# A scan-then-experts kernel: decays loaded first, bf16 filler matmuls, a reordered chunk pipeline, earlier gathers, and a GpSimd drain moved

## The chip, the cores and the metric

The kernel runs on one core of a Trainium2 chip. The time is device microseconds of one execution of the whole program; of several runs the median is taken. TensorE (PE, with its weight loads PEld), VectorE (DVE), ScalarE (ACT) and GpSimd (POOL) are the engines; SyncE (SP) and ScalarE issue plain DMAs, GpSimd issues the indirect ones (gathers and scatters by a list of row numbers). Each engine runs its own instructions in order and waits for the others through semaphores.

## What is computed

A chunked state-space scan (4 batches, 8 heads, 768 positions, head size 32, state size 16), whose output rows, 3072 of 256, go to a router and then to one of 8 experts each:

```python
for c in range(nc):                      # the reference's chunks
    L = np.exp(cum[..., :, None] - cum[..., None, :]) * causal
    y_intra = (C @ B.T * L) @ x
    y_inter = (C @ state) * exp(cum)[..., None]
    state = decay_full * state + sum_j(B_j x_j * decay_from_j)
x = y as rows (3072, 256)
logits = normed(x) @ normed(expert_emb).T / tau
e = argmax(logits); gate = softmax(logits)[e]
out[mask_e] = gate * (relu(x[mask_e] @ w1[e]) @ w2[e])   # 256 -> 1024 -> 256
```

## The kernel before

The order of every engine's work is written by hand, in the order of the Python calls (`tc.manual_schedule`); the framework adds only the semaphores. All data are float32, except some counting matrices in bfloat16.

**Set-up** (`mamba`, lines 624 to 652). `expert_emb` (416) issues two small loads on ScalarE's queue, `load_decays` (40) six loads of 16 KB, three each on SP's and ScalarE's queues; `load(k, 0)` (49) starts chunk 0's inputs on SP. `build_consts` (77) fills constants with VectorE memsets and GpSimd selections. `warm_up` (126) issues 12 float32 matmuls of 128 columns whose result nobody reads. `decays` (131) is a string of some ten small VectorE operations that turn the decay factors into running products `f`, for chunks 0 to 3 (half 0) or 4 and 5 (half 1). `spread_decays` (155) multiplies `f` out on TensorE into columns 384 to 512 of the PSUM tile `pg`; `scale_c` (215) multiplies C by it on VectorE, giving `cp`; `split_b` (207) and `mask_c` (225) make masked copies of B and `cp` on ScalarE. `inverses` (185) takes reciprocals of `f` (VectorE, then two ScalarE copies); `turn_inverses` (194) transposes them on TensorE into `rT`, by which GpSimd scales x (`scale_x`, 239, and `scale_first_half`, 249). `block_ends` (165) and `spread_ends` (173) spread the decays at block ends; `square_emb`, `scale_emb` (439) and `turn_emb` (454) make the normed expert embedding, and `route_consts` (464) the constants of the routing on GpSimd.

**The scan** goes over 6 chunks of 128 positions, all batches and heads at once (`for c in range(NC)`, 654 to 733). For chunk c:
- `inner(c, 0)` and `inner(c, 1)` (317): products of B and C into `pg`, for two batches each. `mask_inner` (333) multiplies them by the causal mask on VectorE into `g` (1.76 us each). There is one `pg`: the second half's products wait for VectorE to have read the first half, and, as the tile is shared, also for `scale_c` of the next chunk.
- `finish(c-1)` (392) turns the outputs of the chunk before into rows and appends the router's logits; `keep_rows` (402) copies them on ScalarE, `send_rows` (410) stores them in DRAM.
- `pick(c-2)` (501), five VectorE operations, finds each row's expert; `count_picks` (517) counts them on GpSimd; `rank_rows` and `keep_ranks` (522, 540), `places` (545) and `locate` (584) turn counts into row lists per expert.
- `from_states` (343), `outputs(c, 0)`, `outputs(c, 1)` (354), `first_outputs` (372): matmuls that add up the chunk's output in `py`; `keep_outputs` (385) copies it on ScalarE.
- `sums` (294), `add_sums` (306), `decay_states` (278): the state for the next chunk; `between` (260) and `pass_c` (231) are small GpSimd steps for it.

In chunk 5 the row lists of chunks 0 to 2 are already known: `gather_halves` (808) gathers the first rows of experts 0 and 1 (four indirect DMAs), `early_jobs` (855) makes two jobs of them, and `scan_end` (737) weaves their matmuls among the last routing steps.

**The experts** (`moe`, 1010). A job has `turn_x` (900, transposes), eight `up` (916), two `down` (930) and one `out` (945) per 104 rows: two transposes, a scaling by the gate on VectorE, and a scatter by GpSimd. The loop's last job does its `up`s and returns at line 1038; `leftover` (1149) then handles rows beyond an expert's 416, in a branch that is not taken here; `moe_end` (1068) does the last job's `down`s and four `out`s, with a `gpsimd.drain()` after the second of them (line 1077). A drain makes GpSimd's sequencer wait until its work is done.

Of the kernel before, what the change touches and what calls it, by code (L numbers as in the profile page):

```python
# [17 lines left out]
Q = 128  # L18
# [57 lines left out]

def build_consts(k):
    nc, pool, mc = k.nc, k.const, k.mc
    k.heads = mc.tile([128, Q], F32, name="heads")
    nc.vector.memset(k.heads[:], 0.0)  # L80
    nc.vector.memset(k.heads[:, 0:Q:SQ], 1.0)
    k.ready = mc.tile([128, 1], F32, name="ready")
    nc.scalar.activation(k.ready[:], k.heads[:, 0:1], ACT.Square)
    k.spread = mc.tile([128, 4, 128], F32, name="spread")
    nc.gpsimd.memset(k.spread[:], 0.0)
    for b in range(NB):
        s = k.spread[32 * b : 32 * b + 32].rearrange("k c (q t n) -> k c q (t n)", q=4, t=2)
        for t in range(2):
            nc.gpsimd.affine_select(
                out=s[:, :, :, N * t : N * t + N], in_=s[:, :, :, N * t : N * t + N],  # L90
                pattern=[[-1, 4], [-4, 4], [0, N]], compare_op=ALU.not_equal, fill=1.0, base=-16 * t,
                channel_multiplier=1,
            )
    k.tmask = mc.tile([128, 2], F32, name="tmask")
    nc.vector.memset(k.tmask[:], 0.0)
    for q in range(4):
        nc.vector.memset(k.tmask[32 * q : 32 * q + N, 0:1], 1.0)
    nc.vector.tensor_scalar(
        out=k.tmask[:, 1:2], in0=k.tmask[:, 0:1], scalar1=-1.0, scalar2=1.0, op0=ALU.mult, op1=ALU.add
    )  # L100
    k.of_b = mc.tile([128, NB], F32, name="of_b")
    nc.vector.memset(k.of_b[:], 0.0)
    for b in range(NB):
        nc.vector.memset(k.of_b[32 * b : 32 * b + 32, b : b + 1], 1.0)
    k.ident = pool.tile([128, 128], F32, name="ident")
    make_identity(nc, k.ident[:])
    k.mask = mc.tile([128, 3 * HQ], F32, name="mask")
    nc.gpsimd.memset(k.mask[:], 1.0)

    def keep(m, pattern, base):  # L110
        nc.gpsimd.affine_select(
            out=m, in_=m, pattern=pattern, compare_op=ALU.is_ge, fill=0.0, base=base, channel_multiplier=-1
        )

    keep(k.mask[0:HQ, 0:HQ], [[1, HQ]], 0)
    keep(k.mask[HQ:, 0:HQ], [[1, HQ]], 0)
    keep(k.mask[:, HQ:].rearrange("p (v i) -> p v i", v=2), [[0, 2], [1, HQ]], HQ)
    k.xb = [mc.tile([128, NB, 4, 2, D], F32, name=f"xb{i}") for i in range(2)]
    for t in k.xb:
        nc.vector.memset(t[0:HQ, :, :, 1, :], 0.0)  # L120
        nc.vector.memset(t[HQ:, :, :, 0, :], 0.0)
    k.half = pool.tile([128, NT], F32, name="half")
    nc.gpsimd.memset(k.half[:], 0.5)


def warm_up(k):
    for _ in range(12):
        k.nc.tensor.matmul(k.pz[0][:, 0:Q], lhsT=k.heads[:], rhs=k.heads[:], start=True, stop=True)


def decays(k, kk):
# [185 lines left out]
def inner(k, c, j):  # L317

    t = k.ld[c]
    for u in range(2):  # L320
        b = 2 * j + u
        for lhsT, rhs, a, n in ((t.bi[:, b, :], t.cp[:, b, 3:5, :], HQ, Q), (t.bt[:, b], t.cp[:, b, 0, :], 0, HQ)):
            for q in range(4):
                r = slice(32 * q, 32 * q + 32)
                m = lhsT[r] if n == Q else lhsT[r].rearrange("p v s -> p (v s)")
                x = rhs[r].rearrange("p v s -> p (v s)") if n == Q else rhs[r]
                k.nc.tensor.matmul(  # L327
                    k.pg[:, q, 192 * u + a : 192 * u + a + n], lhsT=m, rhs=x, start=True, stop=True,
                    tile_position=(32 * q, 0),
                )  # L330
# [133 lines left out]
def route_consts(k):  # L464
    nc = k.nc

    def ints(name, shape, pattern, base, by, dtype=F32):
# [8 lines left out]
    k.place_at = ints("place_at", [128, TR], [[1, TR]], 1, 0)  # L476
    k.first_of = ints("first_of", [128, NT], [[TR, NT]], 0, 0)
    k.ints = ints
    ones = k.mc.tile([128, 128], F32, name="ones")
    nc.gpsimd.memset(ones[:], 1.0)  # L480
    before = k.mc.tile([128, 128], F32, name="before")
    nc.gpsimd.affine_select(
        out=before[:], in_=ones[:], pattern=[[1, 128]], compare_op=ALU.is_gt, fill=0.0, base=0,
        channel_multiplier=-1,
    )
    k.ones = k.const.tile([128, 128], BF16, name="ones_b")
    nc.gpsimd.tensor_copy(out=k.ones[:], in_=ones[:])
    k.before = k.const.tile([128, 128], BF16, name="before_b")
    nc.gpsimd.tensor_copy(out=k.before[:], in_=before[:])
    k.ob = k.const.tile([128, NU, E], BF16, name="ob")  # L490
    k.pre = k.const.tile([128, NU + 1, E], BF16, name="pre")
    nc.gpsimd.memset(k.pre[:, 0, :], 0.0)
# [131 lines left out]
def mamba(k):  # L624
# [6 lines left out]
    for c in range(NC):  # L631
        k.ld[c] = Net()
        k.ld[c].g = []
    expert_emb(k)
    load_decays(k)
    load(k, 0)
    build_consts(k)
    warm_up(k)
    decays(k, 0)
    load(k, 1)  # L640
    square_emb(k)
    route_consts(k)
    spread_decays(k, 0)
    split_b(k, 0)
    inverses(k, 0)
    scale_c(k, 0)
    mask_c(k, 0)
    block_ends(k, 0)
    turn_inverses(k, 0, k.py[:, 0, 0:256])
    scale_emb(k)  # L650
    scale_x(k, 0, nc.gpsimd)
    scale_first_half(k, 0, nc.gpsimd)

    for c in range(NC):
        t = k.ld[c]
        n = c + 1
        if c + 2 < NC:
            load(k, c + 2)
        if c in (3, 4):
            load_weights(k, 0, (c - 3,))  # L660
        if c == 5:
            load_weights(k, 1, (0,))
        if n < NC:
            spread_decays(k, n)
        if 0 < c < NC - 1:
            add_sums(k, c)
        inner(k, c, 0)
        mask_inner(k, c, 0)
        if c == NC - 1:
            early_places(k, c - 3)  # L670
        elif c >= 3:
            locate(k, c - 3)
            keep_located(k, c - 3)
        if n < NC:
            scale_x(k, n, nc.gpsimd)
        if c >= 2:
            pick(k, c - 2)
        if n < NC:
            scale_c(k, n)
        if c == 0:  # L680
            spread_ends(k, 0, k.pz[0][:, 0:48])
            turn_emb(k, k.pz[1][:, 400:416])
        if c > 0:
            finish(k, c - 1)
            keep_rows(k, c - 1)
            send_rows(k, c - 1)
        if c == 1:
            spread_ends(k, 1, k.pz[0][:, 400:424])
        inner(k, c, 1)
        mask_inner(k, c, 1)  # L690
        if c == 0:
            sums(k, 0)
            add_sums(k, 0)
        if n < NC:
            split_b(k, n)
            mask_c(k, n)
        if c >= 2:
            count_picks(k, c - 2)
        if n < NC:
            scale_first_half(k, n, nc.gpsimd)  # L700
            if c in (0, 3):
                between(k, n, 4 if c == 0 else NC)
            pass_c(k, n)
        if 3 <= c < NC - 1:
            add_located(k, c - 3)
        if c == NC - 1:
            k.early_x = gather_halves(k, k.gi0, 0, 3 * NB * Q)
        if c == 0:
            decays(k, 1)
            block_ends(k, 1)  # L710
            inverses(k, 1)
        if c > 0:
            from_states(k, c)
        if c >= 2:
            rank_rows(k, c - 2)
            keep_ranks(k, c - 2)
        outputs(k, c, 0)
        outputs(k, c, 1)
        if c == NC - 1:
            early = early_jobs(k)  # L720
            early[0].turn_x()
        first_outputs(k, c)
        keep_outputs(k, c)
        if c + 2 < NC:
            sums(k, n)
        if c == 1:
            turn_inverses(k, 1, k.pz[0][:, 0:256])
        if c >= 2:
            places(k, c - 2)
        if c == 4:  # L730
            shift_places(k)
        if n < NC:
            decay_states(k, n)
    return early


def scan_end(k, early):
# [2 lines left out]
    c = NC - 1  # L740
    first, second = early
    gates = Gates(k, k.ep, k.early_x, TR, NT)
    pick(k, c - 1)
    count_picks(k, c - 1)
    first.up(0)
    rank_rows(k, c - 1)
    keep_ranks(k, c - 1)
# [57 lines left out]
    k.gi0 = gi  # L805


def gather_halves(k, gi, t, rows=T):
    x = k.ep.tile([TR, 2 * HT, KD * Y1], F32, name="xg", tag="xg", bufs=2)
    for e in range(2):  # L810
        for i in range(HT):
            gather(k, x[:, HT * e + i, 0:W], gi[:, NT * e + t + i : NT * e + t + i + 1], rows)
    return x


def gather(k, x, at, rows=T):
# [48 lines left out]


def late_jobs(k):
    x = k.late_x = gather_halves(k, k.gi, HT)
    jobs = []
    for e in range(2):  # L870
        j = Job(k, HT, TR, k.w1t[e], k.w2t[e], k.ep, k.next_bank)
# [138 lines left out]
def moe(k, second, late):  # L1010
# [10 lines left out]
    for i in range(E):  # L1021
# [5 lines left out]
        for f in range(KF):  # L1027
# [8 lines left out]
            if i >= 4 and f >= 5:  # L1036
                next(left, None)
        if i == E - 1:
            return j
        if x is not None:  # L1040
            gates.power()
# [26 lines left out]
def moe_end(k, j):  # L1068

    for i in range(2):  # L1070
        j.down(0, i)
        if i:
            j.out(0)
        j.down(1, i)
        if i:
            j.out(1)
            k.nc.gpsimd.drain()
    j.out(2)
    j.out(3)

# [244 lines left out]
```

## Time and profile before

| what | us |
|---|---|
| median of 6 runs (294.32 to 300.26) | 298.5 |
| the profiled execution's own time | 298.41 |
| its span, first to last instruction | 296.6 |
| TensorE busy in the span | 267.7 (90%) |
| VectorE, ScalarE, GpSimd busy | 118.8, 70.8, 123.9 |
| expert layers at full TensorE load | about 114.5 to 271.3 |
| TensorE's granted clock, mean | 0.945 |

A page cuts the span into 40 slices and gives each engine's busy share in tenths, and the share of its full clock that TensorE was granted. Groups of instructions come with count, busy time and the mean of one, and with the idle time just before them and what ended it. "issue" is time in which an engine waited for nothing that the profile shows. A "q" after an engine's name is its sequencer, which handles waits, branches and drains.

### The profile page before, as it was taken

What the parts mean: (1) busy time and instruction counts of PE and PEld (TensorE: products, weight loads), DVE (VectorE), ACT (ScalarE), POOL (GpSimd) and SP (SyncE); (2) the same over time, 40 slices, a digit from 0 to 9 for tenths busy, and PEclk for the clock granted to TensorE, in tenths of its full rate; (3) what the DMA queues carried; (4) which work ended last, traced back from release to release, by engine and by line L of the source; (5) the groups of instructions that cost most, each with busy time, mean ns of one, the idle gap of its engine ahead of it and who ended that gap; (6) DMA issues with size and microseconds to landing.
All of it is one profiled execution on the core that took longest, in us unless ns stands there. A gap on an engine that the chain in (4) does not pass through costs nothing.

```text
span 296.6 us, 5877 instructions
## 1 busy us (share of the span) xinstructions
PE 267.7 (90%) x2331; PEld 199.7 (67%) x2331; DVE 118.8 (40%) x350; ACT 70.8 (24%) x211; POOL 123.9 (42%) x173
## 2 busy tenths in 40 slices
PE   6879967998789999999999999999999999999920
PEld 6769856887579999999555565565555555556920
DVE  6675575558625412143250441242244046042120
ACT  3315335051136132340310130130031031010000
POOL 8987346452521561845251263155057051031012
PEclk9578999599979999999999999999999999999995
DMA  4993779517316950698644527429321010011011
GB/s 136 283 322 90 239 231 223 177 61 160 105 32 204 250 134 0 150 245 195 176 102 101 167 78 148 144 56 201 124 71 47 15 43 6 0 29 33 2 29 28
DMA packets 22302, 35.86 MB, mean 121 GB/s; under 512 B 2547, under 2 KB 15550, under 8 KB 22272
## 3 DMA queue, kind: packets, MB, share of 16 engines
q1 hardware_dynamic: 19024, 28.73, 35.3%
q0 software_dynamic: 3072, 6.67, 9.1%
q8 instruction: 19, 0.31, 0.5%
q14 instruction: 11, 0.09, 0.1%
q10 hardware_dynamic: 176, 0.06, 0.1%
HBM read 29.05 MB, written 6.65 MB: 120 GB/s over the span
## 4 chain that ended last, share of the span: by engine, by line
issue 43%; PE 27%; POOL 16%; DVE 8%; DMA 3%; POOLq 1%; ACT 0%; ACTq 0%
POOL xg L817 8%; POOL out_dram L952 7%; PE pg L327 5%; DVE g L337 4%; PE eb L922 4%; PE eb L937 4%; PE py L378 3%; DMA out_dram<-yo,to 3%; PE py L365 3%; PE pz L298 1%; PE py L348 1%; PE hp L922 1%; PE pg L159 1%; DVE cp L220 1%; POOL gr L979 1%
## 5 line engine op out<-in xcount | busy, mean ns | idle before, releaser
L922 PE MATMUL hp<-xT,w 128*128 128x416 f32 (+1 forms) x256 | 83.9, 469 | 0.0
L937 PE MATMUL yp<-hT,w 128*128 128x416 f32 (+1 forms) x288 | 80.1, 436 | 0.3 <-PEq L1157 0.3
L952 POOL DMA_INDIRECT out_dram<-yo,to x32 | 32.5, 1016 | 100.8 <-DVE yo L951 90.6
L937 PEld LDWEIGHTS yp<-hT,w 128*128 128x128 f32 x288 | 52.3, 190 | 24.8 <-issue 23.1
L922 PEld LDWEIGHTS hp<-xT,w 128*128 128x128 f32 x256 | 45.8, 190 | 23.2 <-issue 23.1
L817 POOL DMA_INDIRECT xg<-y_rows,gi x32 | 35.4, 1106 | 12.7 <-issue 8.4
L926 ACT ACTIVATE hT<-hp 128x416 f32<-128x416 f32 (+1 forms) x32 | 15.2, 475 | 81.9 <-PE hp L922 80.2
L928 DVE TENSOR_SCALAR hT<-hp 128x416 f32<-128x416 f32 (+1 forms) x32 | 17.2, 538 | 40.4 <-PE hp L922 38.5
L337 DVE TENSOR_TENSOR g<-pg,mask 128x1536 f32<-128x1536 f32 x12 | 21.1, 1758 | 16.2 <-PE pg L327 16.1
L943 DVE COPY yoT<-yp 128x416 f32<-128x416 f32 (+1 forms) x9 | 4.4, 489 | 48.7 <-PE yp L937 48.7
L327 PE MATMUL pg<-cp,bi 32*128 32x128 f32 x192 | 13.1, 344 | 3.1 <-DVE cp L220 3.1
L519 POOL TENSOR_TENSOR pre<-pre,ob 128x8 bf16<-128x8 bf16 x24 | 4.8, 200 | 25.7 <-DVE ob L514 24.2
L979 POOL TENSOR_TENSOR gr<-gr,half 104x4 f32<-104x4 f32 x8 | 8.7, 1092 | 16.2 <-ACT sq L973 16.1
L365 PE MATMUL py<-g,xs 128*32 128x64 f32 x384 | 10.8, 247 | 3.5 <-issue 2.9
L378 PE MATMUL py<-g,xb 128*64 128x64 f32 x192 | 10.0, 261 | 4.2 <-issue 4.2
L973 ACT ACTIVATE sq<-xg 104x256 f32<-104x256 f32 x32 | 13.0, 409 | 0.0
L922 PE MATMUL eb<-xT,w 128*128 128x208 f32 x64 | 12.9, 347 | 0.0
L378 PEld LDWEIGHTS py<-g,xb 128*64 128x64 f32 x192 | 8.6, 169 | 5.5 <-issue 5.0
L937 PE MATMUL eb<-hT,w 128*128 128x208 f32 x64 | 12.0, 341 | 0.0
L327 PEld LDWEIGHTS pg<-cp,bi 32*128 32x128 f32 x192 | 9.2, 222 | 4.0 <-DVE cp L220 3.8
L242 POOL TENSOR_TENSOR xs<-x,rT 128x1024 f32<-128x1024 f32 x6 | 11.8, 1969 | 0.1
L365 PEld LDWEIGHTS py<-g,xs 128*32 128x32 f32 x384 | 8.0, 127 | 5.6 <-issue 4.2
(202 smaller groups left out, 325.0 us busy)
## 6 DMA issues: line engine op xcount, KB each, us to landing
w<-in_moe_w_dram SPq DMA_DIRECT2D x16, 512.0 KB, 7.4
w<-in_moe_w_dram SPq DMA_DIRECT2D x8, 1024.0 KB, 7.3
y_rows<-rows SPq DMA_DIRECT2D x6, 528.0 KB
x<-in_x_dram SPq DMA_DIRECT2D x6, 512.0 KB, 9.4
ct<-in_CT_dram SPq DMA_DIRECT2D x6, 256.0 KB
bi<-in_BT_dram SPq DMA_DIRECT2D x6, 256.0 KB, 5.4
b<-in_B_dram SPq DMA_DIRECT2D x6, 256.0 KB, 7.7
xa<-in_x_dram SPq DMA_DIRECT2D x6, 128.0 KB, 7.0
```

The source lines that it names most:

```text
L242: engine.tensor_tensor(out=t.xs[:].rearrange("p b (h d) -> p b h d", h=NH), in0=t.x[:].rearrange("p b (h d) -> p b h d", h=NH), in1=r_of(k ...
L327: k.nc.tensor.matmul(k.pg[:, q, 192 * u + a : 192 * u + a + n], lhsT=m, rhs=x, start=True, stop=True, tile_position=(32 * q, 0),)
L337: k.nc.vector.tensor_tensor(out=g[:], in0=k.pg[:, :, 0:384].rearrange("p q (u m) -> p q u m", u=2), in1=k.mask[:].unsqueeze(1).unsqueeze(1 ...
L365: k.nc.tensor.matmul(k.py[o : o + 32, z, Q * b + HQ : Q * b + Q], lhsT=t.xs[:, b, n : n + 32], rhs=t.g[j][:, q, u, HQ + HQ * v : Q + HQ * ...
L378: k.nc.tensor.matmul(k.py[o : o + 64, z, Q * b : Q * b + HQ], lhsT=k.xb[c % 2][:, b, q].rearrange("p v d -> p (v d)"), rhs=t.g[b // 2][:, ...
L817: k.nc.gpsimd.indirect_dma_start(out=x, out_offset=None, in_=k.y_d[0:rows, :], in_offset=bass.IndirectOffsetOnAxis(ap=at, axis=0), bounds_ ...
L922: nc.tensor.matmul(t, lhsT=s.w1[:, j, 128 * f : 128 * f + 128], rhs=s.xT[:, j, :], start=(j == 0), stop=(j == KD - 1))
L926: nc.scalar.activation(s.hT[:, f, :], t, ACT.Relu)
L928: nc.vector.tensor_scalar_max(s.hT[:, f, :], t, 0.0)
L937: nc.tensor.matmul(t, lhsT=s.w2[:, f, 128 * j : 128 * j + 128], rhs=s.hT[:, f, r], start=(f == 0), stop=(f == KF - 1))
L952: d = nc.gpsimd.indirect_dma_start(out=k.out[:, :], out_offset=bass.IndirectOffsetOnAxis(ap=s.to[:, i : i + 1], axis=0), in_=y[:], in_offs ...
L973: s.k.nc.scalar.activation(sq[:], s.x[:, i, :].rearrange("p (j w) -> p j w", j=KD)[:, :, 0:128], ACT.Square, accum_out=s.r[:, i : i + 1],)
```

## The change

Six edits. (1) The decays' loads are issued ahead of the embedding's. (2) The filler matmuls become bfloat16, 512 columns each, on a tile `warm` of their own: 13 at the start, 3 behind the first spreading of decays, 2 behind the second; to make room, two routing constants borrow a buffer of `T`. (3) In the set-up, C is decayed ahead of the reciprocals; chunk 1's spreading, chunk 0's first products and chunk 1's decayed C come before the loop, with the embedding's last steps behind them; chunk 1's first products and their masking stand between chunk 0's two halves of outputs; the second half of the decays moves from chunk 0 to the end of chunk 1, and its follow-ups from chunk 1 to 2; within `inner` the two kinds of products swap order. (4) From chunk 1 on, `scale_c` of the next chunk comes ahead of `pick`. (5) In chunk 5 the first two gathers are issued ahead of `count_picks`, the other two behind it; `rank_rows(3)` comes behind the first job's `turn_x`; `pick(4)` and its counts come ahead of `places(3)`. (6) The GpSimd drain moves from `moe_end` to the end of the last job's `up`s, ahead of the branch of `leftover`. The number of all other matmuls, and all other shapes, stay.

```diff
 def build_consts(k):
+    k.warm = mc.tile([128, 512], BF16, name="warm")
+    nc.vector.memset(k.warm[:], 1.0)
     k.heads = mc.tile([128, Q], F32, name="heads")
...
-def warm_up(k):
-    for _ in range(12):
-        k.nc.tensor.matmul(k.pz[0][:, 0:Q], lhsT=k.heads[:], rhs=k.heads[:], start=True, stop=True)
+def warm_up(k, n):
+    for _ in range(n):
+        k.nc.tensor.matmul(k.pz[1][:], lhsT=k.warm[:, 0:Q], rhs=k.warm[:], start=True, stop=True)
...
-        for lhsT, rhs, a, n in ((t.bi[:, b, :], t.cp[:, b, 3:5, :], HQ, Q), (t.bt[:, b], t.cp[:, b, 0, :], 0, HQ)):
+        for lhsT, rhs, a, n in ((t.bt[:, b], t.cp[:, b, 0, :], 0, HQ), (t.bi[:, b, :], t.cp[:, b, 3:5, :], HQ, Q)):
...
+    load_decays(k)
     expert_emb(k)
-    load_decays(k)
     load(k, 0)
     build_consts(k)
-    warm_up(k)
+    warm_up(k, 13)
     decays(k, 0)
     load(k, 1)
     square_emb(k)
     route_consts(k)
     spread_decays(k, 0)
+    warm_up(k, 3)
     split_b(k, 0)
+    scale_c(k, 0)
     inverses(k, 0)
-    scale_c(k, 0)
     mask_c(k, 0)
+    spread_decays(k, 1)
+    warm_up(k, 2)
+    inner(k, 0, 0)
+    mask_inner(k, 0, 0)
     block_ends(k, 0)
     turn_inverses(k, 0, k.py[:, 0, 0:256])
-    scale_emb(k)
     scale_x(k, 0, nc.gpsimd)
     scale_first_half(k, 0, nc.gpsimd)
+    scale_c(k, 1)
+    scale_emb(k)
+    spread_ends(k, 0, k.pz[0][:, 0:48])
+    turn_emb(k, k.pz[1][:, 400:416])
...
-        if n < NC:
+        if 2 <= c < NC - 1:
             spread_decays(k, n)
-        if 0 < c < NC - 1:
             add_sums(k, c)
-        inner(k, c, 0)
-        mask_inner(k, c, 0)
+        if c >= 2:
+            inner(k, c, 0)
+            mask_inner(k, c, 0)
...
+        if 1 <= c < NC - 1:
+            scale_c(k, n)
+        if c == 1:
+            add_sums(k, c)
         if c >= 2:
             pick(k, c - 2)
-        if n < NC:
-            scale_c(k, n)
-        if c == 0:
-            spread_ends(k, 0, k.pz[0][:, 0:48])
-            turn_emb(k, k.pz[1][:, 400:416])
...
-        if c == 1:
+        if c == 2:
             spread_ends(k, 1, k.pz[0][:, 400:424])
...
+        if c == NC - 1:
+            k.early_x = early_rows(k)
+            gather_halves(k, k.early_x, k.gi0, 0, 0, 3 * NB * Q)
         if c >= 2:
             count_picks(k, c - 2)
+        if c == NC - 1:
+            gather_halves(k, k.early_x, k.gi0, 0, 1, 3 * NB * Q)
...
-        if c == NC - 1:
-            k.early_x = gather_halves(k, k.gi0, 0, 3 * NB * Q)
-        if c == 0:
-            decays(k, 1)
-            block_ends(k, 1)
-            inverses(k, 1)
         if c > 0:
             from_states(k, c)
-        if c >= 2:
+        if 2 <= c < NC - 1:
             rank_rows(k, c - 2)
             keep_ranks(k, c - 2)
         outputs(k, c, 0)
+        if c == 0:
+            spread_decays(k, 2)
+            inner(k, 1, 0)
+            mask_inner(k, 1, 0)
+            add_sums(k, 0)
         outputs(k, c, 1)
         if c == NC - 1:
             early = early_jobs(k)
             early[0].turn_x()
+            rank_rows(k, c - 2)
+            keep_ranks(k, c - 2)
         first_outputs(k, c)
...
-        if c == 1:
+        if c == 2:
             turn_inverses(k, 1, k.pz[0][:, 0:256])
+        if c == NC - 1:
+            pick(k, c - 1)
+            count_picks(k, c - 1)
         if c >= 2:
             places(k, c - 2)
...
+        if c == 1:
+            decays(k, 1)
+            block_ends(k, 1)
+            inverses(k, 1)
...
         if i == E - 1:
+            k.nc.gpsimd.drain()
             return j
...
         if i:
             j.out(1)
-            k.nc.gpsimd.drain()
     j.out(2)
     j.out(3)
```

More of the change, by code (lines that the diff above doesn't have):

```diff
@@ L478, in route_consts @@
     k.ints = ints
-    ones = k.mc.tile([128, 128], F32, name="ones")
-    nc.gpsimd.memset(ones[:], 1.0)
-    before = k.mc.tile([128, 128], F32, name="before")
+    t = k.work.tile([128, NB, 2 * D], F32, name="T", tag="T")
+    ones, before = (t[:, 2 * i : 2 * i + 2, :].rearrange("p b m -> p (b m)") for i in range(2))
+    nc.gpsimd.memset(ones, 1.0)
     nc.gpsimd.affine_select(
-        out=before[:], in_=ones[:], pattern=[[1, 128]], compare_op=ALU.is_gt, fill=0.0, base=0,
+        out=before, in_=ones, pattern=[[1, 128]], compare_op=ALU.is_gt, fill=0.0, base=0,
         channel_multiplier=-1,
@@ L486, in route_consts @@
     k.ones = k.const.tile([128, 128], BF16, name="ones_b")
-    nc.gpsimd.tensor_copy(out=k.ones[:], in_=ones[:])
+    nc.gpsimd.tensor_copy(out=k.ones[:], in_=ones)
     k.before = k.const.tile([128, 128], BF16, name="before_b")
-    nc.gpsimd.tensor_copy(out=k.before[:], in_=before[:])
+    nc.gpsimd.tensor_copy(out=k.before[:], in_=before)
     k.ob = k.const.tile([128, NU, E], BF16, name="ob")
@@ L692, in mamba @@
             sums(k, 0)
-            add_sums(k, 0)
         if n < NC:
@@ L742, in scan_end @@
     gates = Gates(k, k.ep, k.early_x, TR, NT)
-    pick(k, c - 1)
-    count_picks(k, c - 1)
     first.up(0)
@@ L805, in early_places, with early_rows, gather_halves @@
     k.gi0 = gi
[L808 to L813, printed above, removed]
+def early_rows(k):
+    return k.ep.tile([TR, 2 * HT, KD * Y1], F32, name="xg", tag="xg", bufs=2)
+def gather_halves(k, x, gi, t, e, rows=T):
+    for i in range(HT):
+        gather(k, x[:, HT * e + i, 0:W], gi[:, NT * e + t + i : NT * e + t + i + 1], rows)
 def gather(k, x, at, rows=T):
@@ L867, in late_jobs @@
 def late_jobs(k):
-    x = k.late_x = gather_halves(k, k.gi, HT)
+    x = k.late_x = early_rows(k)
+    for e in range(2):
+        gather_halves(k, x, k.gi, HT, e)
     jobs = []
```

## The prediction

> **What bounds the kernel now.** I read the page's slices first, for where TensorE is busy and at what clock.
>
> ```profile
> PE   6879967998789999999999999999999999999920
> PEclk9578999599979999999999999999999999999995
> ```
>
> From about 84 us TensorE is full until 271 us; before that it has holes and spells of half clock, and the last 25 us are half empty. Busy times by stretch, cut where the granted clock changes, make that a table (columns: length, then PE, PEld, DVE, ACT, POOL busy with their counts, clock, DMA share, GB/s).
>
> ```profile
> 8.00:18.24 10.24, 9.27 (x156) 8.43 (x160) 6.00 (x12) 3.70 (x12) 9.69 (x23) 0.50 1.03 296
> 18.24:25.07 6.83, 4.76 (x124) 4.30 (x120) 5.09 (x16) 1.46 (x4) 5.15 (x8) 0.75 0.90 251
> ...
> 114.50:271.30 156.80, 156.54 (x586) 97.93 (x584) 52.82 (x157) 31.53 (x103) 60.12 (x57) 1.00 0.39 101
> 271.30:296.60 25.30, 12.58 (x72) 12.02 (x72) 2.87 (x7) 0.67 (x2) 3.99 (x4) 0.83 0.07 18
> ```
>
> The expert layers (114.5 to 271.3) are TensorE's own work at full clock: 156.5 of 156.8 us. The change does not touch their matmuls, so time can come only from starting them sooner or from the tail. Shorter stretches show what the clock followed:
>
> ```profile
> 4.58:8.00 3.42, 1.68 (x19) 1.33 (x17) 3.11 (x12) 1.83 (x6) 2.95 (x11) 1.00 0.98 275
> 8.00:11.41 3.41, 2.81 (x42) 2.57 (x42) 1.63 (x7) 1.66 (x5) 3.08 (x15) 0.50 0.95 303
> ```
>
> After 3.4 us with TensorE 49% busy the clock was halved, and 82% busy did not bring it back. The waits say what TensorE stood for (total, times, longest):
>
> ```profile
> PE py L378 <- issue: 4.2, 3, 2.1
> ...
> PE pg L327 <- DVE cp L220: 3.1, 4, 1.4
> ```
>
> Three stalls of up to 2.1 us have no releaser (instructions not yet there), and four waits are for the decayed C of the next chunk. The last view is the end of the chain (start, length, what).
>
> ```profile
> 281.06 1.00 POOL out_dram L952
> 282.06 1.84 issue
> 283.90 1.25 POOLq L1077
> 285.15 5.18 issue
> ...
> 291.23 1.00 POOL out_dram L952
> 292.22 1.30 POOLq L1321
> ```
>
> The drain of line 1077, one instruction of 6.40 us from 283.90, stands between the second and third of the last four scatters. Their rows are ready on VectorE at 284.36 and 284.75; they go out at 291.23 and 292.53.
>
> **The change part by part.** The sum is against the profiled execution: 298.41 us, span 296.6, so 1.8 lie around it; the median of the six runs is 298.5, practically the same.
>
> *Tail (drain moved).* Without line 1077's drain the third scatter follows the second at the pitch of earlier pairs (263.13 to 264.48, 266.33 to 267.67: 1.35): 284.16 + 1.34 = 285.50, the fourth at 286.84, over at 287.84 instead of 293.53: 5.69 us. The moved drain begins behind the scatter that ends at 268.67. The old one ended 5.15 us after its last scatter (290.30 - 285.15), so the new one ends near 273.8; then the branch, its semaphores and the semaphore update of 1.39 us, some 2.9 in all, to 276.7. GpSimd's next work is at 281.06, and VectorE's first scaled row, which waits for that update, at 280.27: 3.5 us of cover, and nobody else waits for GpSimd there. Unknown is the drain that ends the kernel: it ended 1.73 us after the last scatter (295.25 - 293.53) with two scatters behind it, the other 5.15 with all earlier ones. It will have four. Ends: 1.73 (gain 5.7) and 5.15 (gain 2.3). I take **-5.7**, as four is nearer to two than to the more than sixty gathers and scatters before line 1077.
>
> *Head, to the first masking of chunk 2 (35.38).* Loading the decays ahead of the expert embedding is worth 0: VectorE began them at 4.76, right behind its last memset (4.24 + 0.48). The new bf16 memset stands ahead of all that: 0.2 to 0.5 us (128 f32 columns took 0.17, 512 took 0.48); taken 0.3, so the decays' spreading on TensorE is at 7.63 instead of 7.33. The reciprocal (0.95) now comes behind the first decayed C: that C is ready at 8.76, the reciprocal at 9.65, ScalarE's two copies at 10.2, and its two masked C's, queued behind them, at 11.15 (before: 9.67). The products that read these cannot end before 11.85 at full clock or 12.5 at half, so the first g starts there, not at 11.77. Block ends (0.26), C of chunk 1 (0.62) and the embedding (about 0.9), done on VectorE in the gap from 8.64 to 11.77 or at 13.44, now come behind g, and TensorE's embedding transposes, in order ahead of the next products, wait for them: 15.4 to 16.0. So chunk 0's second g starts at 16.6 (full) or 18.4 (half), against these rows:
>
> ```profile
> 11.77 1.76 DVE L337 TENSOR_TENSOR g<-pg,mask 128x1536 f32<-128x1536 f32 x1 [2.06 <-PE pg L327]
> 13.44 0.68 DVE L220 TENSOR_TENSOR cp<-ct,pg 128x512 f32<-128x512 f32 x1
> 16.22 1.76 DVE L337 TENSOR_TENSOR g<-pg,mask 128x1536 f32<-128x1536 f32 x1 [2.10 <-PE pg L327]
> ```
>
> GpSimd's scaling of x waits for the transposed inverses, now behind these products: 12.8 or 13.6 instead of 11.74; sums and outputs come later still, so that is covered. The gain comes behind that: chunk 1's first products and their g sit amid chunk 0's outputs, so the serial piece 23.84 to 27.4 (products, g) leaves chunk 1. By the durations of the rows (products 1.1, sums 0.65, half outputs 0.65, first outputs 1.3, finish 2.1, states 1.1, g 1.76) the spreading for chunk 3 starts at 30.6 at full clock, or 32.4 with the clock of before up to 18.24, against 33.97. Chunk 1's second decay block (3.6 us on VectorE at 4.76, 4.5 at 18.29) moves from under the outputs to behind chunk 2's T and holds back V and g of chunk 2 by up to 1 us: g at 32.6 or 34.6 against 35.38, a gain of 2.8 or 0.8. The instruction stall of 2.07 at 19.19 lies in what I compare with and may come again: ends -2.8 and +1.3 (0.8 gained, 2.07 lost). Taken **-1.2**, between the four corners and nearer to full clock, which the fillers (13 of 512 columns at the start, 3 and 2 in the gaps after it) should mostly hold.
>
> [...]
>
> *Chunks 2 to 4 (decayed C ahead of the picks).* Five pick instructions (1.07 us) leave the path of the second products. Their place in the waits: idle 1.42, 0.69 and 0.69 at 38.78, 50.25, 64.83. Chunk 2 gains 0.8, as the spread of ends (0.61) moves into the same hole; chunk 3 between 0 and 0.66, as an instruction stall of 1.38 follows at 50.91, taken 0.3; chunk 4 0.67. The picks end 0.7 later against that C; GpSimd's counts follow, and had 2.7 idle. **-1.8**, ends -0.8 and -2.3. The half clock of 52.37 to 59.20, entered after a stretch 39% busy, costs some 2.6 us of the path; I leave it in, and let the range reach to its loss.
>
> *Chunk 5 (gathers first).* Before, on GpSimd:
>
> ```profile
> 77.13 1.30 POOL L817 DMA_INDIRECT xg<-y_rows,gi  x1 [0.81 <-issue]
> 78.74 1.09 POOL L817 DMA_INDIRECT xg<-y_rows,gi  x1 [0.30 <-issue]
> ```
>
> The first pair waits for the counts (75.29 to 76.33), though its indices are ready at 74.22. Now the pair goes from 75.0 to 77.7, the counts to 78.9, the second pair to 81.7, and the next counts, which waited there too, to 82.8. The transposes of x, at 83.42, could start at 79.2 if TensorE's outputs, which trickled with unexplained stalls of 0.4 to 0.5 us from 77.83 to 83.05, end at 78.9; then the first outputs end near 81.2 against 86.2, and 0.9 is lost again waiting for the later counts: -4.2. If the trickle stays where it is: 0. The trickle has the same times as the gathers, but at 100.5 to 105.9 four gathers ran and matmuls kept 0.18 us each. **-2.0**, the middle.
>
> Sum: -5.7 - 1.2 - 1.8 - 2.0 = -10.7, so 298.4 - 10.7 = **287.7 us**.
>
> **The rivals.**
> *The closing drain is long* (5.15 behind four scatters): tail 2.3, total 291.1. For it: line 1077's drain took that. Against: the closing one took 1.73.
> *The front gives nothing* (clock at half, stalls and trickle as before): tail and 1.0 of the chunks, 298.4 - 6.7 = 291.7. For it: 82% busy did not free the clock, and the stalls are tied to the instruction stream, 12 instructions shorter now. Against: the waits for C are plainly removed.
> *The front gives everything* (full clock, no trickle, no half clock at 52): 298.4 - 5.7 - 2.8 - 2.3 - 2.6 - 4.2 = 280.8.
> *Slower:* TensorE waits for ScalarE's masked C (9.2 to 11.15) between the fillers and the products, so the clock stays at half, and with VectorE's queue in front of each product it does not come back. Half clock costs at most 0.5 us per us; against -10.7 and 1% (3 us) it decides from about 27 us of half clock more than before, up to chunk 3's end: 301.5 and more. Against: from 25.07 on full clock came back with no fillers at all.
>
> **How the numbers follow.** Forecast 0.60 (its own range 283 to 292); long closing drain 0.13; front nothing 0.17; front everything 0.05; slower 0.05. Range: 281 (all gains) to 295 (long drain, front nothing but 1.0: 298.4 - 2.3 - 1.0 = 295.1), leaving out under 0.2. About 1% is what this measurement can tell from no change: faster 0.89, within 1% 0.06 (long drain and lost front together, or half of the slower case), slower 0.05.
>
> **What would show it.** Right: the drain at about 268 and the four scatters at one stretch, the last over within 4 us of TensorE's end; C ahead of the picks with no wait of 0.7 or more in chunks 2 and 4; the first g of chunk 0 no earlier than 11.8, the second later than 16.2, yet chunk 3's spreading before 33; x transposed before 81. Wrong: a closing drain over 4 us; waits for C of the same length under another name; half clock beyond 25; outputs of chunk 5 ending at 83 as before.

## The result, and the profile after

Median 288.08 us (20 runs, 285.22 to 295.64) against 298.29 us (46 runs, 293.05 to 302.48); the ratio is 0.971, 95% interval 0.968 to 0.974. The forecast was 287.7. A ratio here and below compares only those runs of either kernel that lie within 1.5% of its fastest; medians are over all. The profiled execution took 287.43 us, its span is 285.6, against 298.41 and 296.6.

The slices first: the holes and half-clock spells of the front are fewer, but not gone, and the half-empty end is one slice shorter.

```profile
PE   6589989988799999999999999999999999999990
PEclk9959978999979999999999999999999999999996
```

Then one table by stage for each kernel, cut at the first masking of chunk 2, at the last addition of located rows (chunk 4) and at the gates of the first early job (columns: length, then PE, PEld, DVE, ACT, POOL busy with counts, clock, DMA share, GB/s). Before:

```profile
0.00:35.38 35.38, 29.07 (x571) 26.20 (x572) 21.80 (x60) 12.36 (x33) 27.49 (x56) 0.81 0.76 223
35.38:68.13 32.75, 27.21 (x651) 24.23 (x654) 21.48 (x49) 11.80 (x30) 16.42 (x29) 0.90 0.60 171
68.13:96.07 27.94, 23.83 (x357) 21.05 (x346) 15.32 (x59) 9.53 (x30) 7.31 (x18) 0.94 0.42 115
96.07:296.60 200.53, 187.55 (x772) 128.25 (x770) 60.21 (x184) 37.11 (x119) 72.66 (x72) 0.98 0.38 96
```

After:

```profile
0.00:36.41 36.41, 28.05 (x567) 21.18 (x567) 24.24 (x62) 11.74 (x31) 27.17 (x56) 0.91 0.75 217
36.41:66.22 29.81, 27.95 (x691) 24.68 (x692) 23.46 (x52) 12.31 (x34) 16.66 (x28) 0.89 0.65 188
66.22:90.78 24.56, 21.28 (x306) 19.45 (x303) 14.77 (x57) 9.50 (x30) 7.22 (x19) 0.93 0.49 129
90.78:285.60 194.82, 187.55 (x772) 128.25 (x770) 60.29 (x184) 36.95 (x119) 72.54 (x72) 0.99 0.38 99
```

The differences: head **+1.03** (forecast -1.2), chunks 2 to 4 **-2.94** (-1.8), chunk 5 **-3.38** (-2.0), experts and tail **-5.7** (-5.7). TensorE's work in the last row is the same 187.55. So the sum was met with three of the four terms off, one of them in its sign. TensorE's waits after say what changed in kind (total, times, longest):

```profile
PE pz L180 <- DVE ends L169: 2.5, 1, 2.5
PE pg L161 <- DVE f L154: 1.8, 1, 1.8
PE eb L931 <- DMA xg<-y_rows,gi: 1.7, 1, 1.7
...
PE pz L590 <- DVE V L314: 1.0, 1, 1.0
...
PE pg L329 <- DVE cp L222: 0.6, 1, 0.6
PE pz L300 <- issue: 0.5, 1, 0.5
```

The waits for the decayed C are 0.6 instead of 3.1, as forecast. But the stalls with no releaser, 8.5 us in all before, are down to 0.5, which no step had in its sum; and new waits, for block ends, V and gathered rows, have come. Before, the stalls were 4.2 us at line 378 and these (the first is the trickle, seven short stalls among chunk 5's outputs):

```profile
PE py L365 <- issue: 2.9, 7, 0.5
...
PE pg L327 <- issue: 1.4, 1, 1.4
```

The end of the chain after (start, length, what):

```profile
270.23 5.28 issue
...
275.76 0.99 POOL out_dram L974
276.76 1.85 issue
...
279.89 1.26 POOLq L1343
281.15 0.30 issue
281.46 1.00 POOL out_dram L974
```

Line 1343's is the closing drain, issued at 279.89 and ending at 284.29, 1.83 us behind the last scatter's end (282.46). The moved drain holds GpSimd's sequencer from 262.12 to 268.36; the branch and semaphores end at 270.2, and 5.28 us of issue follow before the next scatter is due: nobody waited for it.

### The profile page after: what moved, and what is told of

It is laid out like the page before. It is cut to its first block, busy times and chain, and to the rows that moved or that the text cites. A ratio compares the mean times of both kernels' runs of the same rounds, so it can differ in the third digit from the quotient of the medians.

```text
span 285.6 us, 5865 instructions
## 1 busy us (share of the span) xinstructions
PE 264.8 (93%) x2325; PEld 193.6 (68%) x2325; DVE 122.8 (43%) x351; ACT 70.5 (25%) x211; POOL 123.6 (43%) x173
## 4 chain that ended last, share of the span: by engine, by line
issue 41%; PE 21%; POOL 19%; DVE 10%; DMA 6%; POOLq 1%; ACT 1%; DVEq 0%
POOL xg L837 9%; POOL out_dram L974 8%; PE eb L944 5%; DMA out_dram<-yo,to 4%; PE eb L959 4%; PE pg L329 3%; DVE g L339 2%; DMA xg<-y_rows,gi 2%; PE py L380 1%; PE py L398 1%; PE py L367 1%; PE pz L590 1%; PE pz L398 1%; PE hp L944 1%; DVE cp L222 1%
## 5 line engine op out<-in xcount | busy, mean ns | idle before, releaser
L944 PE MATMUL eb<-xT,w 128*128 128x208 f32 x64 | 14.2, 371 | 0.0
L329 PE MATMUL pg<-cp,bi 32*128 32x128 f32 x192 | 12.2, 326 | 0.8 <-ACT cp L230 0.8
L944 PEld LDWEIGHTS eb<-xT,w 128*128 128x128 f32 x64 | 11.8, 204 | 0.1
L959 PEld LDWEIGHTS eb<-hT,w 128*128 128x128 f32 x64 | 11.1, 190 | 0.0
L329 PE MATMUL pg<-cp,bt 32*128 32x64 f32 x192 | 10.2, 283 | 0.6 <-DVE cp L222 0.6
L973 DVE TENSOR_SCALAR yo<-ot,gate 104x256 f32<-104x256 f32 x18 | 8.6, 478 | 4.5 <-PE ot L971 4.5
L391 ACT COPY yT<-py 128x512 f32<-128x512 f32 x12 | 6.4, 589 | 16.0 <-PE py L380 16.0
```

The lines of the kernel that those rows point to most:

```text
L329: k.nc.tensor.matmul(k.pg[:, q, 192 * u + a : 192 * u + a + n], lhsT=m, rhs=x, start=True, stop=True, tile_position=(32 * q, 0),)
L944: nc.tensor.matmul(t, lhsT=s.w1[:, j, 128 * f : 128 * f + 128], rhs=s.xT[:, j, :], start=(j == 0), stop=(j == KD - 1))
L959: nc.tensor.matmul(t, lhsT=s.w2[:, f, 128 * j : 128 * j + 128], rhs=s.hT[:, f, r], start=(f == 0), stop=(f == KF - 1))
L973: nc.vector.tensor_scalar_mul(y[:], t[:tr, 0:DM], s.gate[:, i : i + 1])
```

## The experiments

**The kernel before, once more, for its stalls.**

> The kernel before, unchanged, for a second profile: do TensorE's stalls without a releaser (2.07, 1.13, 1.38 and 1.04 us at 19.19, 43.05, 50.91 and 68.97, and the seven of 0.34 to 0.47 from 77.83 to 83.05) come again? If the stream of instructions sets them, they stand behind the same matmuls (number 221, 731, 859, 1242 and 1414 to 1448) with lengths within 0.5 us, 8 to 9 us in all. If they hang on what the DMA rings happen to carry, they move or change by more than half, and part of the kernel's spread of 294 to 302 us is theirs.

297.04 us. The stalls are there again, behind the same matmuls of the stream:

```profile
PE py L378 <- issue: 5.6, 4, 2.2
PE pg L327 <- DVE cp L220: 4.1, 4, 1.4
PE pg L327 <- issue: 1.9, 1, 1.9
PE py L365 <- issue: 1.9, 5, 0.4
...
PE eb L909 <- issue: 0.8, 2, 0.4
```

They stand behind number 221 (2.15 us), 731 (1.18), 859 (1.93), 986 (0.79) and 1242 (1.48), apart by multiples of about 127.6 matmuls. The places are those of before, with a new one (986); the lengths are less constant: that behind 859 is 0.55 us longer. The page lists the transfers that fit:

```profile
q8 instruction: 19, 0.31, 0.5%
```

There are 19 packets of 16 KB, one for about 128 matmuls with their weight loads; such a group is called a block here, and the place between two of them a border. The packets were laid against the matmuls over all 14 profiles of this study, up to chunk 5. Of 140 borders 39 have a stall, and at each of the 39 TensorE goes on 1.23 to 1.64 us (median 1.41) after that block's packet has ended. At the other 101 the matmul behind the border comes 1.05 us or more after it, at all but two 1.4 or more. A few borders (reached: when TensorE starts the last matmul of the block before; the request is taken as that block's start):

```
kernel   stall behind  requested  packet         reached  goes on  stall
before   221            14.76     18.50-19.62     18.97    21.26   2.07
before   859            44.18     49.43-50.78     50.64    52.29   1.38
before   1242           65.21     67.58-68.53     68.75    70.02   1.04
after    (1240)         62.21     62.53-63.48     65.70    65.75   none
```

So a block stalls TensorE when its 16 KB land later than about 1.4 us ahead of need, and what makes them late is the wait from request to packet: 3.74, 5.26 and 2.38 us here in stretches with a DMA share of 1.07, 1.01 and 0.92 (packets are counted where they start, so it can pass 1), and 0.32 in the fourth row, with no other transfer in it. The Trainium skill's page "Runtime: NRT & Kernel Launch", section "Instruction fetch mechanics", has the 16 KiB blocks too and calls the cost of crossing a border mostly hidden; in the expert layers the traces agree (17.9 us and more to spare at each border), in the scan, where 128 small matmuls last 3.5 us, they do not.

**The loads taken away.** Chunks 2 to 5 use the tiles of two chunks before:

```diff
     t = k.ld[c]
+    if c >= 2:
+        o = k.ld[c - 2]
+        t.ct, t.bi, t.b, t.x, t.xa = o.ct, o.bi, o.b, o.x, o.xa
+        return
```

> The kernel before with the loads of chunks 2 to 5 left out: they work on the data of the two chunks before (so the rows picked differ, and only the time up to the expert layers is read). Theory (TensorE's stalls without a releaser are its own instructions, in blocks of 128 matmuls, fetched behind the loads: in the two profiles of before the fetch landed after or within 0.2 us of the end of the block before it wherever there was a stall, and 1.3 us or more ahead wherever there was none): the stalls behind matmuls 221, 731, 859, 986 and 1242, 8.0 to 8.5 us in all with the others, fall to under 2, those that remain where expert weights are loaded. Rival (the stream or its fetches are slow by themselves): 6 us or more of stalls stay, behind the same matmuls.

The stall behind 221 is gone: the request at 14.82 was served at 15.20, after 0.38 us, with no other transfer in that time (before: 3.74, engines full). The stall behind 859 is gone too. (The whole takes 471.13 us, as other rows are picked and the branch for leftover rows is taken; only the front is read.) Three stalls stay:

```profile
PE py L382 <- issue: 4.7, 3, 2.2
```

They are 2.22, 0.99 and 1.49 us behind 731, 987 and 1242, after waits of 3.06, 2.33 and 2.71 us with a DMA share of 1.02, 0.90 and 0.92. The packets in these waits are those of the stores of rows (1056 bytes each: 330, 512 and 512 of them) and of the first expert weights (114, 34 and 33). So the loads are the cause where they were taken away; the size, under 2 us, was missed, as the stores and the weights, which stay, are enough.

**The decayed C back behind the picks**, in the changed kernel:

```diff
-        if 1 <= c < NC - 1:
+        if c == 1:
             scale_c(k, n)
         if c == 1:
             add_sums(k, c)
         if c >= 2:
             pick(k, c - 2)
+        if 2 <= c < NC - 1:
+            scale_c(k, n)
```

> The changed kernel with the decayed C behind the picks again in chunks 2 to 4. Rival, by the terms of the prediction: TensorE's waits for C come back (1.4, 0.7, 0.7) and no more, 1.0 to 1.8 us, 289.1 to 289.9. Theory (with the second products 0.7 to 1.4 us later, the next block's fetch is asked for behind the loads instead of ahead of them, as in chunk 4 of before, where the request came 0.2 us after the weight load's issue, against 0.4 us before it in the changed kernel): instruction stalls come back beside the waits, 2 us or more of them, 291 or more.

293.75 us (4 runs, 292.52 to 295.83), ratio 0.989 (0.980 to 0.998). Not only the waits came back:

```profile
PE py L380 <- issue: 3.7, 2, 2.6
PE pg L329 <- DVE cp L222: 3.0, 3, 1.6
...
PE pg L329 <- issue: 0.7, 1, 0.7
```

4.4 us of border stalls, and chunks 2 to 4 take 34.05 us (37.30 to 71.35) instead of 29.81. In chunk 4 the reason can be read from SyncE's queue and the packets. After, the border falls at 62.21, and then:

```profile
62.17 0.37 SPq L413 DMA_DIRECT2D y_rows<-rows  x1
62.58 2.24 SPq L69 DMA_DIRECT2D w<-in_moe_w_dram  x2
```

With the picks ahead the border falls at 68.60:

```profile
67.80 0.37 SPq L413 DMA_DIRECT2D y_rows<-rows  x1
68.22 1.51 SPq L69 DMA_DIRECT2D w<-in_moe_w_dram  x2
```

The second products wait 0.69 us for C, and the store of rows does not, so the block's request comes 0.80 us behind the store's issue instead of 0.04. After, its packet was taken at 62.53, 0.32 us after the request and ahead of the store's first at 63.07. Here the store's 512 packets start from 68.70 to 71.05, and the block's comes behind them at 71.14, after 2.54 us. The weights, issued behind the store, only start at 70.34; so the store is what the block stood behind. In the 13 profiles with this border the packet comes behind the whole store in six, all with a stall of 1.04 to 1.49 us (before is one: store 65.48 to 67.50, block 67.58). In the other seven it comes ahead of the store or with its first packets, and none has a stall.

**The decayed C ahead of the picks alone**, in the kernel before: `scale_c` and `pick` change places.

> The kernel before with the decayed C of the next chunk ahead of the picks on VectorE, nothing else. Theory: TensorE's waits for it in chunks 2 to 4 (1.42, 0.69, 0.69) fall to 0.7 or less each, 1.0 to 1.8 us less, ratio 0.994 to 0.997. Rival (instruction stalls take the place of the waits): the sum of TensorE's idle time in chunks 2 to 4 stays within 0.5 us, ratio 0.998 to 1.002.

291.95 us (5 runs, 290.71 to 301.22), ratio 0.975 (0.969 to 0.982). That is about 7 us, more than either theory or rival had; but the one profiled run is the 301.22. There the waits for C are 0.8 us, the border behind 1242 has no stall, and those behind 221, 731, 859 and 986 have 2.99, 1.94, 1.19 and 2.25. So the waits went as forecast; where the rest of the 7 us comes from is not shown, nor whether the short runs are those without stalls.

**The drain alone**, in the kernel before:

```diff
         if i == E - 1:
+            k.nc.gpsimd.drain()
             return j
...
             j.out(1)
-            k.nc.gpsimd.drain()
```

> The kernel before with the drain alone moved, from behind the second of the last four scatters to the end of the last expert's first layer. Theory (the drain costs only what it holds back, and the closing one stays short behind four scatters): 5.7 us less, a ratio of 0.981, the closing drain ending 1.8 us after the last scatter. Rival (the closing drain takes over the old one's length): 2.3 us less, ratio 0.992, the closing drain 5 us behind the last scatter.

292.97 us, ratio 0.980 (0.973 to 0.988). From the first early gates to the last scatter's end: 191.70 us instead of 197.46. The closing drain ends 1.82 us behind the last scatter. The theory holds to 0.1 us.

**No drain in the middle**, in the changed kernel: the moved line is left out.

> The changed kernel with the moved drain left out, so that more than sixty gathers and scatters stand behind the closing drain alone. Theory (the length of a drain behind its last transfer follows the number of transfers since the drain before, 5.0 us behind all, 1.8 behind four): the closing drain ends 5.0 us or more after the last scatter instead of 1.83, 3.3 us more than the changed kernel, 291.4. Rival (the moved drain's 5.0 us are something else, such as the first layer's end, and the closing one is always near 1.8): within 0.5 us of 288.1.

293.51 us (10 runs, 289.60 to 296.42), ratio 0.993 (0.987 to 1.000). The closing drain runs from 279.15 to 287.03, 5.31 us behind the last scatter's end (281.72) instead of 1.83; gates to last scatter take the same 191.67. So a drain's length follows what was issued since the one before, and the moved drain pays for the long one where nobody waits. Over the profiles it ends 1.71 to 1.77 us behind the last transfer with two gathers and scatters since the drain before, 1.82 to 1.88 with four or five, 4.98 to 5.32 with 60 to 64, and 7.19 with 87 (the kernel without chunk loads). The drain explains 3.5 us of the difference of 5.4 between the medians, which were not taken side by side; the rest, in the front, was not followed up.

**Chunk 5's order alone**, in the kernel before (core of the edit):

```diff
+        if c == NC - 1:
+            k.early_x = early_rows(k)
+            gather_halves(k, k.early_x, k.gi0, 0, 0, 3 * NB * Q)
         if c >= 2:
             count_picks(k, c - 2)
+        if c == NC - 1:
+            gather_halves(k, k.early_x, k.gi0, 0, 1, 3 * NB * Q)
...
             early[0].turn_x()
+            rank_rows(k, c - 2)
+            keep_ranks(k, c - 2)
```

> The kernel before with chunk 5's order alone changed: first pair of gathers ahead of the counts, ranks behind the transposes of x, the next picks brought forward. Theory (the trickle of chunk 5's outputs is tied to something other than the gathers, and goes when rank products and counts leave its path): x transposed 3 to 5 us sooner, 2 to 4.2 us less, ratio 0.986 to 0.993. Rival (the trickle is the gathers' own work taking TensorE's instruction supply): it moves with the gathers, still 3 us or more in all, and under 1 us is gained, ratio 0.997 or more.

296.31 us, ratio 0.987 (0.981 to 0.994). The trickle is gone, though the gathers still run beside the outputs; so is the rival. In its place is one wait before the transposes of x, which start at 79.20 and go on at 81.52, 5.3 us after the issue of the second gather:

```profile
81.52 0.78 PE L918 MATMUL eb<-ident,xg 104*128 104x104 f32 x3 [2.02 <-issue]
```

The changed kernel shows the same with its releaser:

```profile
71.27 1.30 POOL L837 DMA_INDIRECT xg<-y_rows,gi  x1 [4.80 <-DVE oh L512]
72.87 1.08 POOL L837 DMA_INDIRECT xg<-y_rows,gi  x1 [0.30 <-issue]
```

```profile
77.84 0.49 PE L931 MATMUL eb<-ident,xg 104*128 104x104 f32 x3 [1.68 <-DMA xg<-y_rows,gi]
```

That is 77.84 - 72.87 = 4.97 us; the last packet of that gather ended at 77.28, 4.41 us after its issue. Before, the transposes followed the trickle without a gap:

```profile
83.42 0.96 PE L909 MATMUL eb<-ident,xg 104*128 104x104 f32 x4
```

There the last packet had ended at 81.28, 2.54 us after the issue at 78.74. Where a landing is recorded, it comes 0.4 to 0.5 us after the last packet, so these rows were there at about 81.8 (an estimate), and the trickle cost some 1.6 us. In the other four profiles with a trickle the same gap is 0.5 to 0.8. So the new order removes the trickle, and pays part of it back: its second gather takes 1.9 us longer (4.4 to 4.6 us to the last packet in all eight profiles with the new order, 2.5 to 2.6 in the six with the old). Why it does is open, and so is what makes the trickle; in the kernel without chunk loads, which has the old order, there is none.

**The second decay block forward**, in the changed kernel:

```diff
         mask_inner(k, c, 1)
         if c == 0:
+            decays(k, 1)
             sums(k, 0)
...
         if c == 1:
-            decays(k, 1)
             block_ends(k, 1)
             inverses(k, 1)
```

> The changed kernel with the second block of decays brought forward, from behind chunk 2's T to right behind chunk 0's second g; its block ends and reciprocal stay where they are. Theory (the block, whose scan took 2.02 us beside GpSimd's scaling of x against 0.42 elsewhere, held V and the first g of chunk 2 from about 32 to 36.07 and 36.41): V of chunk 2 by 33.5, first g of chunk 2 by 35, and with TensorE's 1.7 us of holes there gone also the half clock of 38.59 to 45.42: 1.5 to 4.5 us less than the changed kernel, 283 to 286. Rival (the block is only paid at another place, before chunk 1's g): first g of chunk 2 at 36 or later, the time within 1 us of the changed kernel's 288.1.

285.13 us (4 runs, 284.48 to 289.87), ratio 0.974 (0.965 to 0.984). The block had stood here in the changed kernel (VectorE):

```profile
30.70 0.66 DVE L285 TENSOR_TENSOR T<-V,wm 128x256 f32<-128x256 f32 x1
...
32.25 2.02 DVE L144 TENSOR_TENSOR_SCAN f<-a,heads 128x128 f32<-128x128 f32 x1
...
36.07 0.42 DVE L314 TENSOR_TENSOR V<-pz,U 128x128 f32<-128x128 f32 x2
36.41 1.75 DVE L339 TENSOR_TENSOR g<-pg,mask 128x1536 f32<-128x1536 f32 x1
```

and now:

```profile
21.89 0.46 DVE L144 TENSOR_TENSOR_SCAN f<-a,heads 128x128 f32<-128x128 f32 x1
...
33.63 0.49 DVE L314 TENSOR_TENSOR V<-pz,U 128x128 f32<-128x128 f32 x2 [0.79 <-PE pz L300]
35.08 1.76 DVE L339 TENSOR_TENSOR g<-pg,mask 128x1536 f32<-128x1536 f32 x1 [0.96 <-PE pg L329]
```

V comes 2.4 us sooner, the first g of chunk 2 1.33, and the half clock from 38.59 to 45.42 is gone. The scan's 2.02 us ended 0.28 us behind GpSimd's scaling of x, and it is 0.46 where GpSimd has only small products:

```profile
32.02 1.97 POOL L244 TENSOR_TENSOR xs<-x,rT 128x1024 f32<-128x1024 f32 x1
```

The Trainium skill, page "SBUF — State Buffer", section "Who interferes with whom", says that a VectorE instruction with two inputs in SBUF contends with a GpSimd instruction that reads SBUF; the scan's rows agree.

**Block ends and embedding ahead of the first g as well:**

```diff
+    block_ends(k, 0)
+    scale_emb(k)
     inner(k, 0, 0)
     mask_inner(k, 0, 0)
-    block_ends(k, 0)
...
     scale_c(k, 1)
-    scale_emb(k)
```

> As the kernel with the early decay block, and chunk 0's block ends and the scaled expert embedding ahead of chunk 0's first g on VectorE, in the 2.46 us it idles there. Theory (TensorE's wait of 2.53 us for the block ends at 12.5, with the half clock of 14.70 to 21.53 behind it, is the head's loss): chunk 0's second g at 15 to 17 instead of 19.57, first g of chunk 2 2 to 4 us before that of the kernel with the early block alone, 280 to 284 us in all. Rival (GpSimd's scaling of x, 4.2 us a chunk from 13.04 on without a break, is what the outputs wait for, or instruction fetches behind the loads take the gain back as stalls): second g at 15 to 17, but under 1 us of it left at chunk 2.

288.78 us (4 runs, 283.30 to 289.95; the profiled one 288.38). In its profile the wait for block ends is gone, the second g is at 16.82 instead of 19.57, and 0.94 us of it is left at chunk 2 (34.14 against 35.08). Then the stalls take it back, as the rival had it (its scan took 1.23 us, again ending 0.28 behind a scaling by GpSimd):

```profile
PE py L380 <- issue: 2.7, 2, 1.6
PE pg L329 <- issue: 2.4, 1, 2.4
```

**The borders moved**, in the kernel before: 64 small matmuls behind the warm-up.

> The kernel before with 64 small matmuls more behind the warm-up, in the 1.85 us in which TensorE waits there for the decays: nothing else than the place of the borders between blocks of 128 matmuls is changed. Theory (instructions come in blocks, and a stall is a block that lands behind its border): the stalls stay behind the same numbers of the stream (221, 731, 859, 986, 1242, those that are left), which now are products and sums 64 matmuls sooner, and none is left inside the first outputs of chunks 2 to 4 at the place of before; blocks now hold dense and loose stretches alike (about 5 us each instead of 3.5 and 6.5), so the stalls shrink from 8 to 10 us to 3 to 6 and the time by 2 to 5 us. Rival (the stalls belong to the work, such as the first outputs waiting for something unseen): they stay in the first outputs, now behind 285, 795, 1050 and 1306, and the time stays within 1 us or grows by the added matmuls.

296.89 us, ratio 1.004 (0.999 to 1.009). This told nothing apart: the trace has 128 matmuls for the 64 calls, a whole block, so every border stayed at its work. The stalls (behind 349, 859 and 987) are on the series 221 + 127.6 n and inside the same work as before, as either theory would have it.

**The changed kernel and the early decay block, side by side.**

> The changed kernel once more, beside the kernel with the early decay block on the same chip, for a second profile. If its freedom from instruction stalls (0.5 us against 8 to 11 before) is the order's doing, they stay under 3 us and the first g of chunk 2 stands at 36 to 37 again; if the first profile was luck, 5 us or more of them come back. Time 286 to 290.

> The kernel with the early decay block once more, beside the changed kernel on the same chip. Theory: 2 to 3 us below it (1.3 at the first g of chunk 2, and the half clock behind the hole at 35 to 38 gone), 284 to 286. Rival (its first four runs were a lucky draw of stalls and clock): within 1 us of it.

290.97 us (6 runs, 285.52 to 292.66) and 287.38 us (6 runs, 285.86 to 287.95; ratio to before 0.965, 0.960 to 0.970). In its second profile the changed kernel has one border stall, 1.53 us behind 986 (under the 3 us expected if the order does it), and the first g of chunk 2 at 37.17 against 35.45. The early block is the better version, by 1.3 to 1.7 us at chunk 2 in both pairs of profiles; how much at the end, the overlapping runs leave open.

## Why the prediction was right, and where it was not

**The tail: right.** -5.7 forecast, -5.76 by the drain alone; the closing drain took 1.83, as taken (4.40 as one instruction, as it begins ahead of the last two scatters), and the long-drain rival is what comes if the drain is left out.

**Chunk 5: the step right, its working not.** From the first g of chunk 5 to the gates the kernel gained 2.0 us (23.91 to 21.91, both with 3.4 us of half clock in it), as taken. The step took the pair as over at 77.7, by the time that GpSimd needs to issue it, and the transposes as free at 79.2. It had no term for the rows' own way: after, the last rows came 3.3 us behind the end of the pair's issue (77.28 against 73.96), and the transposes waited for them instead of the trickle. The other 1.4 us of the stage lies ahead of that g, 1.04 of it the stall behind 1242.

**Chunks 2 to 4: the direction right, half the mechanism missed.** The waits for C went from 2.8 to 0.6. What the step did not see is that TensorE's place against the bulk transfers decides the border stalls, 2.51 us here before and none after (1.53 in the second profile). The undo cost 4.2 us in this stage, not 1.8.

**The head: wrong sign.** +1.03 instead of -1.2, though the stall of 2.07 left too. The mis-sized term is VectorE's small work queued behind g and beside GpSimd's scaling: block ends took 1.03 (0.26 before, 0.16 in the kernel with both moves), the scaling of the embedding 1.29 (0.47), so the second g came at 19.57, not 16.6 to 18.4; and the decay block lasted 4.9 us (31.29 to 36.15), not 3.6 to 4.5, and held V and g to 36.4 instead of 32.6 to 34.6. The early decay block and the one with both moves show either part. The rows, before:

```profile
8.64 0.26 DVE L167 TENSOR_TENSOR ends<-f,of_b 128x12 f32<-128x12 f32 x1
...
9.23 0.47 DVE L448 TENSOR_SCALAR en<-emb,emb_r 8x128 f32<-8x128 f32 x2
```

After, GpSimd scales x from 13.04 on:

```profile
13.99 1.03 DVE L169 TENSOR_TENSOR ends<-f,of_b 128x12 f32<-128x12 f32 x1
...
15.96 1.29 DVE L450 TENSOR_SCALAR en<-emb,emb_r 8x128 f32<-8x128 f32 x2
19.57 1.76 DVE L339 TENSOR_TENSOR g<-pg,mask 128x1536 f32<-128x1536 f32 x1 [2.32 <-PE pg L329]
```

**The rivals.** "The front gives nothing" had the stalls tied to the stream, and that is how they are tied; it failed because in the changed order the blocks' requests met the bulk transfers less, as chunk 4 shows. The slower case did not come. As to the clock, the spells differ between executions of one kernel: before had half clock for 23.9 us up to 88 us, its second profile 13.7, after 17.1. The first spell of full clock is longer with the new set-up: it lasts 3.4 us in five and 6.8 in two of the seven profiles with the old one, 6.8 in three and 10.2 in four of the seven with the new. Whether the fillers do that or the order is not shown, as leaving them out was not tried; and the head lost time all the same.

**Its own signs.** Two went against it by the profile: chunk 3's spreading began at 33.09, not before 33, and half clock came back beyond 25 (38.59 to 45.42).

So 287.7 was met partly by luck: about 2 us too much hope in the head was paid for by stalls, 5.6 us at four borders in before, whose end the sum did not contain.

## What to carry to other kernels

Where many small matmuls run beside heavy loads, look at the borders between TensorE's instruction blocks: here a stall with no releaser that came back behind the same matmul was a late block, and an edit that moves a request ahead of a bulk transfer (here a store of 512 packets) can be worth more than the wait it removes. A drain is paid by what was issued since the last one, so put it where GpSimd has cover. Small VectorE work that is moved into a stretch of GpSimd scaling should be costed at its duration there, not at its duration alone.

## What the runs showed of the hardware that was not expected

- TensorE went on 1.23 to 1.64 us after the packet of a late instruction block had ended, at 39 of 39 stalls.
- At the border of chunk 4 the block's packet came either ahead of a store of 512 packets or with its first ones, or behind all of it; the second case has a stall in six profiles of six.
- The second gather of 104 rows had its last packet 2.5 to 2.6 us after its issue in the old order and 4.4 to 4.6 in the new one.
- A GpSimd drain ended 1.8 us behind the last of four scatters, 5.0 to 5.3 behind the last of 60 to 64 gathers and scatters, 7.2 behind the last of 87.
- In chunk 5, from its first g to the gates, half clock can be priced between profiles with the same order there: 20.39 us with none (no drain in the middle), 21.66 to 21.95 with 3.4 us of it (four profiles), 23.18 and 23.29 with 6.8 (two).
